# Batch 2's input stage partly by seven block products, with the sums of w_in moved ahead of it

## The chip, the cores and the metric

One core of a Trainium2 chip. The metric is device time in microseconds (us), the median of several executions. The engines work side by side, each through its own list in order: TensorE (PE) multiplies matrices, VectorE (DVE) and ScalarE (ACT) do element work, GpSimd (POOL) does element work and issues DMAs, SyncE (SP) issues DMAs. Only PE writes matmul results, into eight PSUM banks; DVE and ACT read them out into SBUF, where everything else lies. They wait for each other by semaphores.

## The reference

Attention over 4 batches, 8 heads, 768 positions and 64 columns, with a local window of 16 and, for each block of 32 keys, one summary key (the maximum) and one summary value (the mean). Its output, reshaped to 3072 x 512, goes through a dense layer with a quick GELU. Cut to what matters:

```python
k_sum = k.reshape(B, H, nb, block, D).max(axis=3)
v_sum = v.reshape(B, H, nb, block, D).mean(axis=3)
scores_l = where(|i - j| < 16, scale * q @ k.T, -1e9)
scores_s = scale * q @ k_sum.T + log(32)
a = softmax(concat([scores_l, scores_s]))
x = (a @ concat([v, v_sum])).reshape(3072, 512)
h = x @ w_in                                  # 512 x 2048
return (h * sigmoid(1.702 * h)) @ w_out       # 2048 x 512
```

## The kernel before

The four batches run one after the other. Each has an input stage (x @ w_in and the GELU, giving `gT`: 16 tiles of 128 hidden columns, each for two halves of 384 tokens) and an output stage (`gT` @ w_out). Batch b+1's attention is done inside batch b's output stage: `beside` and the table `plan` say after which of the 21 output products which scores, masks, values and transposes stand.

The order is written out by hand. `_Ordered` wraps every engine and pins each instruction to its place in the program, so every engine's list is the order in which the Python code issues the calls. All instructions therefore carry line 28, and have to be told apart by their tiles.

**The output stage** splits w_out, the hidden columns and the tokens into 2 x 2 blocks and computes the four block results with seven products instead of eight (`product`, steps 1 to 7, for three token columns t of 128; `seq` is their order). This needs sums of blocks of `gT` (`g_sums`, four sums `which` 0 to 3 for a pair of tiles j and j+8, into `gs`) and of w_out (`ws`). Evictions: `keep_it` and `give`, on ACT and DVE.

**The input stage** of batches 0 to 2 is plain: for each hidden tile and half, four matmuls of 128x384 (`ff_step`) into a bank of PSUM, then one GELU on ACT (`gelu`). Batch 3's is by seven products for six of eight tile pairs: `win_sum` makes four sums of blocks of w_in (into `wsi`, which lies in the key and query buffers of even batches, `kxs[0]` and `qTs[0]`), `x_sums` four sums of blocks of x (into `xs`, which lies in `vw[0]`), and for each pair j `ff_product` does seven products of two matmuls. Between them stand `ff_copy` "a" (DVE, bank to bank), "s" (ACT, to SBUF), "b" and "c" (DVE, a bank plus the SBUF copy), and four GELUs (`ff_gelu`). `steps` gives the order by slots, and consecutive pairs are seven slots apart. The banks come from `last_bank` by tags A (3 banks), B (1), C (2), E (2).

Since batch 2 is the last even batch, `wsi` and `xs` can be written once its scores and values are done, that is late in batch 1's output stage. Before, the four `win_sum`s stand on DVE at the start of batch 2's input stage (line 1162).

**Also in batch 2's input stage** the keys, values and queries of batch 3 are made ready: on POOL a copy of one column (`gate2`) waits for the last transposed x, then the four DMAs of q are issued (`load_turned`); on SP `xq` transposes q by DMA and `value_rows` copies the halo rows; `vsum` sums the values by blocks on PE (48 small matmuls, `ps_vs`) and DVE copies these sums out; `rest_k` makes the key maxima (`ks`, DVE) and copies them and the halo columns into the key tiles (`key_halos`, `key_rows`, here DVE).

Of the kernel before, what the change touches and what calls it, by code (L numbers as in the profile page):

```python
# [13 lines left out]
ALU = mybir.AluOpType  # L14
# [21 lines left out]
def kernel(  # L36
# [10 lines left out]
    B, H, S, D = q.shape  # L47
# [5 lines left out]
    NP = H // 2  # L53
# [54 lines left out]
    def load_turned(x, b, t2, name, gs_=(0, 1)):  # L108

        for g in gs_:  # L110
            t2[g] = castp2.tile([128, 2, NJ, 2, D], BF16, name=name, tag=name)
            for hh in range(2):
                h0 = hh * NP + 2 * g
                pool.dma_start(out=t2[g][:, :, :, hh].rearrange("p i a d -> p (i a) d"),
                               in_=x[b, h0:h0 + 2].rearrange("h (a p) d -> p (h a) d", p=128))
# [145 lines left out]

    vs_ps = [None]

    def vsum(s):

        if s:
            big = psb.tile([128, 1024], F32, name="ps_vs", tag="big")
            ps = [big[:, 0:512], big[:, 512:1024]]
        else:
            ps = [pmm.tile([128, 512], F32, name="ps_vs", tag="mm") for e in range(2)]  # L270
        vs_ps[0] = ps
        w5 = vw[s].rearrange("p (j e) h c -> p j e h c", e=2)
        for j in range(NJ):
            o = EX - 4 * j
            for g in range(4):
                for e in range(2):
                    pe.matmul(out=ps[e][32 * g:32 * g + 32, 0:2 * D],
                              lhsT=E[e * 64:e * 64 + 64, o:o + 32],
                              rhs=w5[e * 64:e * 64 + 64, j, e, 2 * g:2 * g + 2, 0:D],
                              start=(j == 0), stop=(j == NJ - 1), skip_group_check=True)  # L280
# [348 lines left out]
    def gelu(half, nt, ph):  # L629
        act.activation(out=gT[half][:, nt, :], in_=ph, func=ACT.Gelu_apprx_sigmoid)  # L630
# [3 lines left out]
    def ff_step(ph, half, nt, steps=range(KO)):  # L634
        for n in steps:
            g, i = n // 2, n % 2
            ko = g + 2 * i if halves[0] else 2 * g + i
            pe.matmul(out=ph, lhsT=w_in_sb[:, ko, nt * 128:(nt + 1) * 128],
                      rhs=xTT[half][g][:, i], start=(n == 0), stop=(n == KO - 1))
# [26 lines left out]
        gelu(half, nt, ph)  # L666


    def g_sums(j, eng=dve, which=(0, 2, 1, 3), m=1):

        js = slice(j, j + m)
        a1, a2 = gTb[:, js], gTb[:, j + NT // 2:j + NT // 2 + m]
        l, r = slice(0, HALF), slice(HALF, S)
        for w in which:
            a, b_, op = {0: (a1[:, :, r], a2[:, :, r], ALU.add), 1: (gs[:, 0, js], a1[:, :, l], ALU.subtract),
                         2: (a1[:, :, l], a1[:, :, r], ALU.subtract),
                         3: (a2[:, :, l], gs[:, 1, js], ALU.subtract)}[w]
            eng.tensor_tensor(out=a1[:, :, r] if w == 2 else gs[:, min(w, 2), js], in0=a, in1=b_, op=op)

    N1 = d_model // 2  # L680

# [19 lines left out]
           .rearrange(two, k=2) for i in range(4)]  # L701
    xs = [vflat[:, i * 2 * HALF:(i + 1) * 2 * HALF].rearrange(two, k=2) for i in range(4)]

    def win_sum(what):

        n = NT // 2 * 128
        k1, k2 = w_in_sb[:, K1], w_in_sb[:, K2]
        a11, a12, a21, a22 = k1[:, :, 0:n], k2[:, :, 0:n], k1[:, :, n:], k2[:, :, n:]
        a, b_, op = {0: (a21, a22, ALU.add), 1: (wsi[0], a11, ALU.subtract),
                     2: (a11, a21, ALU.subtract), 3: (a12, wsi[1], ALU.subtract)}[what]  # L710
        dve.tensor_tensor(out=wsi[what], in0=a, in1=b_, op=op)

    def x_sums():

# [6 lines left out]
    def last_bank(tag, name):  # L721
        return plast[tag in "AB"].tile([128, 512], F32, name=name, tag="last" + tag,
                                       bufs={"A": 3, "E": 2, "B": 1, "C": 2}[tag])
# [325 lines left out]
            else:  # L1049
                tx(half, i, XE.get((half, i), act))  # L1050

    def value_rows(s):
        w5 = vw[s].rearrange("p (j e) h c -> p j e h c", e=2)
        halo_dmas(w5, 0)
        vsum(s)
        block_sums()
        sum_dmas(w5, 0)

# [77 lines left out]
    def run1(steps):  # L1136

        for what in steps.split():
# [9 lines left out]
            else:  # L1148
                g_sums(i)

    XB = {0: 'A4 v0 v1 a4 a5 x0 a6 x1 a7 a8', 2: 'b0 b1 z0 b2 b3 z1', 4: 'b4 b5 z2', 6: 'b6 b7 z3', 8: 'b8 a9 b9 z4'}
    for b in range(0, B - 1):
        nxt = b + 1 < B
        s = (b + 1) % 2
        if b == 1:
            mid.close()
            mid = ExitStack()
            pmm = mid.enter_context(tc.tile_pool(name="pmm", bufs=4, space=bass.MemoryType.PSUM, reuse_waits="tile"))
        if b:
            halves[0] = True  # L1160
            if b == B - 2:
                for w in range(4):
                    win_sum(w)
            for n in range(0, NT, 2):
                if b == 1 and n in XB:
                    run1(XB[n])
                elif n == 0:
                    ff_open(0, order2[0:4], None)
                elif n == 2:
                    for nt in order2[0:4]:  # L1170
                        ff_one(1, nt)
                    g_sums(0)
                    g_sums(1)
                else:
                    for nt in order2[n:n + 2]:
                        for half in range(2):
                            ff_one(half, nt)
                        if b == 1 and n + 2 == NT and nt == order2[n]:
                            value_rows(s)
                    g_sums(n // 2, dve, (0, 1) if n + 2 == NT else (0, 1, 2, 3))  # L1180
                if nxt:
                    if n == 0 and b > 1:
                        pool.tensor_copy(out=gate2, in_=xTT[1][1][:, 1, 0:1])
                        load_turned(q, b + 1, qb2, "qb")
                    if b > 1 and n // 2 == 1:
                        xq(0, s)
                        value_rows(s)
                    if b == 1 and n // 2 in (0, 1):
                        xq(n // 2, s)
                    if b > 1 and n // 2 == 2 * b:  # L1190
                        xq(1, s)
                    p = n // 2 - (3 if b == 1 else 2)
                    if 0 <= p < NP:
                        rest_k(p, s, pool if b == 1 else dve)
        if nxt:
            if b:
                exp_soon()
            beside(b + 1, -1)
        i = 0
        for t, what in seq if b else seq0:  # L1200
            product(b, t, what)
            if i == (2 if b else 0):
                g_sums(NT // 2 - 1, dve, (2, 3))
            if nxt:
                beside(b + 1, i)
            i += 1
            if nxt and b + 2 < B:
                if i == 1 and b:
                    load_batch(b + 2)
                if b and i in (16, 18):  # L1210
                    xk(i // 2 - 8, b % 2)

    mid.close()
    mid0.close()
    for ab in (True, False):
        plast[ab] = ctx.enter_context(tc.tile_pool(name=f"plast{ab:d}", bufs=2, space=bass.MemoryType.PSUM,
                                                   reuse_waits="tile"))
    b, n = B - 1, NT // 2
    PLAIN = 2

    def plain(nt, half, tag):
        ph = last_bank(tag, "ph")[:, 0:HALF]
        ff_step(ph, half, nt)
        gelu(half, nt, ph)

    def ff_do(j, what):
        if isinstance(what, int):
            ff_product(j, what)
        elif what in "asbc":
            ff_copy(j, what)  # L1230
        elif what == "g":
            g_sums(j, pool, (0, 1))
        else:
            ff_gelu(j, what)

    for i, tag in enumerate("CCEEAAA"):
        plain((0, n, 1, n + 1)[i % 4], i // 4, tag)
        if i == 3:
            x_sums()
        if i in (5, 6):  # L1240
            g_sums(0, pool, (0, 1) if i == 5 else (2, 3))
    steps = {0: [1, "a"], 1: [5, "s"], 9: [7, "c"], 10: [3], 4: [2], 5: [6, "b"], 13: [4],
             6: ["C"], 11: ["B"], 12: ["E"], 14: ["A"], 15: ["g"]}
    for slot in range(7 * (n - PLAIN)):
        if slot == 1:
            plain(n + 1, 1, "B")
# [53 lines left out]
```

## Time and profile before

| | us |
|---|---|
| median of 3 runs | 207.48 (207.39 to 207.54) |
| the profiled execution | 207.41 |
| its span, first to last instruction | 205.4 |
| batch 2's input stage, first ph to first scores | 120.53 to 142.07 |
| batch 2's output stage | 142.07 to 164.54 |
| batch 3's input stage to the first output product | 164.54 to 182.64 |

How to read it: times are from the start of the span. A row of the chain of waits has a start, a length and the piece of work that the end depended on. A row of the timeline has a start, a length, the engine, the operation, its output and inputs with their shapes, and in brackets the engine's idle time before it and what ended it. PE's rows overlap, since a matmul's end is 0.16 us after the next one's start. The granted TensorE clock was 1.000 throughout.

```profile
120.53:142.07 21.54, 21.54 (x179) 12.81 (x177) 19.85 (x57) 15.24 (x32) 4.79 (x5) 1.00 1.67 164
142.07:164.54 22.47, 22.47 (x362) 19.34 (x361) 14.66 (x32) 12.15 (x21) 0.00 (x0) 1.00 0.41 85
164.54:182.64 18.10, 18.04 (x113) 10.76 (x111) 11.08 (x21) 14.85 (x35) 13.03 (x15) 1.00 0.13 38
```

These are three stretches of the span (start:end, length), with the busy time of PE, PE's weight loads, DVE, ACT and POOL in each, and then the granted clock, the share of the DMA engines and GB/s. They are the input and output stage of batch 2 and the input stage of batch 3.

### The profile page before, as it was taken

How to read it: one execution, taken by the hardware profiler on the slowest of the kernel's cores; microseconds unless marked ns; L12 is line 12 of the kernel's file. 1: busy time of each engine (PE TensorE's matmuls, PEld its weight loads, DVE VectorE, ACT ScalarE, POOL GpSimd, SP SyncE). 2: the span in 40 equal slices, each digit the busy share in tenths (PEclk: the TensorE clock that was granted, in tenths of full speed). 3: DMA queues.
4: the chain of work that ended last, by engine and by line, in shares of the span. 5: the costliest groups of instructions: out<-in, count | busy, mean ns of one | idle time of the engine just before them, and what ended most of it. 6: DMA issues, size and time to landing. Idle time of an engine off the chain costs nothing.

```text
span 205.4 us, 6003 instructions
## 1 busy us (share of the span) xinstructions
PE 196.9 (96%) x2436; PEld 144.6 (70%) x2436; DVE 142.9 (70%) x369; ACT 130.8 (64%) x253; POOL 100.5 (49%) x159
## 2 busy tenths in 40 slices
PE   7879999999999999999999999999999999999993
PEld 7647556656877776656788875666888865668882
DVE  6956875769998544599877579996768446757221
ACT  2373969769788847776772347778680567984220
POOL 7975389944999423746987044000000009991000
PEclk9999999999999999999999999999999999999999
DMA  5999999999999999999999999999023940000222
GB/s 56 160 156 198 200 209 209 193 158 136 83 164 192 207 189 196 134 126 150 114 165 204 187 155 154 169 210 147 3 102 89 135 140 0 2 3 0 102 105 102
DMA packets 99723, 27.75 MB, mean 135 GB/s; under 512 B 86752, under 2 KB 96752, under 8 KB 99696
## 3 DMA queue, kind: packets, MB, share of 16 engines
q0 software_dynamic: 74064, 13.64, 89.1%
q1 hardware_dynamic: 25632, 13.74, 35.4%
q8 instruction: 19, 0.31, 0.7%
q14 instruction: 8, 0.07, 0.1%
HBM read 27.26 MB, written 6.29 MB: 163 GB/s over the span
## 4 chain that ended last, share of the span: by engine, by line
PE 59%; DMA 15%; POOL 13%; DVE 8%; issue 2%; ACT 0%; POOLq 0%; DVEq 0%
PE poA L28 18%; PE ph L28 16%; DMA qb<-in_q_dram 9%; PE poB L28 9%; DMA w_in_sb<-in_moe_w_in_dram 6%; PE poC L28 4%; PE phA L28 4%; DVE gs L28 4%; POOL kb L28 3%; PE ps_av L28 3%; PE ps_s L28 2%; POOL mk L28 2%; POOL v0n L28 2%; DVE ks L28 2%; POOL qb L28 2%
## 5 line engine op out<-in xcount | busy, mean ns | idle before, releaser
L28 PE MATMUL ph<-xT,w_in_sb 128*128 128x384 f16 x416 | 71.1, 326 | 0.1
L28 PEld LDWEIGHTS <-w_in_sb 128*128 128x128 f16 x452 | 43.3, 98 | 27.6 <-issue 0.5
L28 ACT ACTIVATE gT<-ph 128x384 f16<-128x384 f32 x104 | 49.6, 491 | 18.9 <-PE ph L28 18.6
L28 PEld LDWEIGHTS <-gT 128*128 128x128 f16 x384 | 36.1, 98 | 5.3 <-issue 0.2
L28 POOL DMA_DIRECT2D vw<-in_v_dram x36 | 25.1, 752 | 19.4 <-DMA qb<-in_q_dram 7.5
L28 PEld LDWEIGHTS <-gs 128*128 128x128 f16 x288 | 27.7, 98 | 3.6 <-issue 0.3
L28 ACT ACTIVATE a_sb<-ps_s 128x768 bf16<-128x768 f32 (+1 forms) x32 | 24.8, 826 | 7.8 <-PE ps_s L28 7.8
L28 POOL TENSOR_TENSOR gs<-gT 128x384 f16<-128x384 f16 x7 | 6.4, 910 | 43.7 <-ACT gT L28 43.7
L28 PE MATMUL poA<-ws,gT 128*128 128x256 f16 x192 | 25.1, 273 | 0.1
L28 DVE TENSOR_TENSOR a_sb<-a_sb,mk 128x768 bf16<-128x768 bf16 x28 | 14.6, 554 | 5.5 <-ACT a_sb L28 2.8
L28 POOL DMA_DIRECT2D qb<-in_q_dram x18 | 16.6, 945 | 2.5 <-DMA v0n<-in_v_dram 2.2
L28 DVE TENSOR_TENSOR x<-ps_av,rc 128x768 f16<-128x768 f32 (+1 forms) x20 | 15.8, 797 | 0.6
L28 POOL DMA_DIRECT2D kb<-in_k_dram x16 | 15.3, 973 | 0.8 <-POOLq L1284 0.8
L28 ACT ACTIVATE osb<-poA 128x256 f32<-128x256 f32 x12 | 4.6, 384 | 16.1 <-PE poA L28 16.0
L28 ACT ACTIVATE s<-poA 128x256 f32<-128x256 f32 x17 | 6.5, 384 | 12.6 <-PE poA L28 12.1
L28 DVE TENSOR_TENSOR gs<-gT 128x384 f16<-128x384 f16 (+1 forms) x22 | 8.8, 399 | 8.0 <-ACT gT L28 7.8
L28 PEld LDWEIGHTS <-kx 64*128 64x128 bf16 (+1 forms) x372 | 9.4, 95 | 6.5 <-issue 4.2
L28 ACT ACT_TABLE_LOAD x10 | 12.8, 1283 | 1.0 <-PEq L1284 0.8
L28 PE MATMUL poA<-ws,gs 128*128 128x256 f16 x96 | 12.4, 273 | 0.1
L28 PE MATMUL poA<-w_out_sb,gT 128*128 128x256 f16 x96 | 12.5, 273 | 0.0
L28 PE MATMUL poB<-ws,gs 128*128 128x256 f16 x96 | 12.5, 273 | 0.0
L28 PE MATMUL poC<-w_out_sb,gT 128*128 128x256 f16 x96 | 12.5, 273 | 0.0
(113 smaller groups left out, 299.7 us busy)
## 6 DMA issues: line engine op xcount, KB each, us to landing
out_dram<-osb SPq DMA_DIRECT2D x23, 256.0 KB, 4.1
kb<-in_k_dram POOLq DMA_DIRECT2D x16, 192.0 KB, 7.9
qb<-in_q_dram POOLq DMA_DIRECT2D x14, 192.0 KB, 9.9
vw<-in_v_dram POOLq DMA_DIRECT2D x36, 64.0 KB, 7.1
w_out_sb<-in_moe_w_out_dram POOLq DMA_DIRECT2D x3, 512.0 KB, 10.7
vw<-vs SPq DMA_DIRECT2D x6, 198.0 KB, 5.9
w_in_sb<-in_moe_w_in_dram POOLq DMA_DIRECT2D x4, 256.0 KB, 10.0
w_in_sb<-in_moe_w_in_dram POOLq DMA_DIRECT2D x2, 512.0 KB, 12.0
```

Source lines behind the costliest of these rows:

```text
L28: r = f(*a, **kw)
```

## The change

Batch 2's input stage gets a function of its own, `middle`. Tile pairs 0, 1, 6 and 7 stay plain; pairs 2 to 5 go by seven products, with the helpers of batch 3 and the slot table `steps2`. PSUM is handed out by `last_bank` for this stage, and the pools of before are opened again behind it.

- `win_sum` takes an engine. Its four calls move into batch 1's output stage (`WSUM`): sum 0 on DVE after product 10, sum 2 on POOL after product 13, sum 1 on DVE after 15, sum 3 on POOL after 16. POOL's stand behind batch 3's key and value loads and ahead of the gate copy and the q loads.
- `x_sums` is also called at the start of `middle`, behind the last evictions of batch 1. `value_rows` stands behind the first 16 matmuls and gets two E banks for its sums (`vsum` takes `ps`).
- `rest_k`'s copies go to POOL; the maxima stay on DVE, at the slots in `REST`.
- `g_sums` takes a range of token columns. In `middle` only those of column t = 0 are made (`G0`: pairs 0 and 1, 2 to 4, 5 to 7, all on DVE); those of t = 1 and 2 stand in batch 2's output stage, for all eight pairs at once (`OUTG`, 128x1024 each).
- The lists of ACT and DVE change to match: ACT gets four copies "s", DVE four each of "a", "b" and "c".

```diff
+    OUTG = {1: [(1, 0)], 2: [(1, 1)], 3: [(1, 2)], 4: [(1, 3)], 7: [(2, 0)], 8: [(2, 1)], 9: [(2, 2)], 10: [(2, 3)]}
+    WSUM = {10: [(0, 0)], 13: [(2, 1)], 15: [(1, 0)], 16: [(3, 1)]}
+    LEAD, SEVEN, TAIL = [0, 1], [2, 3, 4, 5], [6, 7]
+    steps2 = {0: [1, "a"], 1: [5, "s"], 4: [2], 5: [6, "b", "C"], 9: [7, "c"], 10: [3], 11: ["B"], 12: ["E"], 13: [4], 14: ["A"]}
+    REST, TAILS, G0 = {6: 0, 12: 1, 20: 2, 27: 3}, {6: 1, 9: 1, 13: 1, 16: 1, 20: 1, 27: 1, 30: 1, 33: 1}, {3: [(0, 2, (0, 2, 1, 3), 0)], 29: [(2, 3, (0, 1), 0)], 31: [(2, 3, (2, 3), 0)], 33: [(5, 3, (0,), 0)], 35: [(5, 3, (1, 2, 3), 0)]}
+
+    def middle(b, s):
+        n = NT // 2
+        pool.tensor_copy(out=gate2, in_=xTT[1][1][:, 1, 0:1])
+        load_turned(q, b + 1, qb2, "qb")
+        tags = iter('CCAACCCB')
+        nts = [nt for j in LEAD for nt in (j, j + n)]
+        phs = {nt: last_bank(next(tags), "ph")[:, 0:HALF] for nt in nts}
+        for part in ((0, 1), (2, 3)):
+            for nt in nts:
+                ff_step(phs[nt], 0, nt, part)
+        for nt in nts:
+            gelu(0, nt, phs[nt])
+        x_sums()
+        xq(0, s)
+        value_rows(s, [last_bank("E", "ps_vs") for e in range(2)])
+        for nt in nts[:-1]:
+            plain(nt, 1, next(tags))
+        more = iter([(h, nt) for j in TAIL for nt in (j, j + n) for h in range(2)])
+        tails = iter('CCCCCCAA')
+        for slot in range(7 * len(SEVEN) + 9):
+            if slot == 1:
+                plain(nts[-1], 1, next(tags))
+            for k_, j in enumerate(SEVEN):
+                for what in steps2.get(slot - 7 * k_, ()):
+                    if what != "g":
+                        ff_do(j, what)
+            for i in range(TAILS.get(slot, 0)):
+                h, nt = next(more)
+                plain(nt, h, next(tails))
+            for j, m, which, eng in G0.get(slot, ()):
+                g_sums(j, (dve, pool)[eng], which, m, 0, 1)
+            if slot in REST:
+                rest_k(REST[slot], s, pool)
+            if slot == 10:
+                xq(1, s)
...
         if b:
             halves[0] = True
             if b == B - 2:
-                for w in range(4):
-                    win_sum(w)
+                mid.close()
+                mid0.close()
+                mid, mid0 = ExitStack(), ExitStack()
+                last_pools(mid)
+                middle(b, s)
...
         for t, what in seq if b else seq0:
             product(b, t, what)
-            if i == (2 if b else 0):
+            if b < B - 2 and i == (2 if b else 0):
                 g_sums(NT // 2 - 1, dve, (2, 3))
+            for t_, w in OUTG.get(i, ()) if b == 2 else ():
+                g_sums(0, dve, (w,), NT // 2, t_, t_ + 1)
+            for w, eng in WSUM.get(i, ()) if b == 1 else ():
+                win_sum(w, (dve, pool)[eng])
             if nxt:
                 beside(b + 1, i)
```

The other lines of the diff make room for this: `vsum` and `g_sums` take their new arguments, `plain`, `ff_do`, `steps` and `last_pools` move up unchanged in what they do, and batch 2's cases leave the common loop over tiles.

More of the change, by code (lines that the diff above doesn't have):

```diff
@@ L262, with vsum @@
     vs_ps = [None]
-    def vsum(s):
-        if s:
+    def vsum(s, ps=None):
+        if ps:
+            pass
+        elif s:
             big = psb.tile([128, 1024], F32, name="ps_vs", tag="big")
@@ L666, in ff_one, with g_sums @@
         gelu(half, nt, ph)
-    def g_sums(j, eng=dve, which=(0, 2, 1, 3), m=1):
+    def g_sums(j, eng=dve, which=(0, 2, 1, 3), m=1, t0=0, t1=JH):
         js = slice(j, j + m)
         a1, a2 = gTb[:, js], gTb[:, j + NT // 2:j + NT // 2 + m]
-        l, r = slice(0, HALF), slice(HALF, S)
+        l, r = slice(t0 * 128, t1 * 128), slice(HALF + t0 * 128, HALF + t1 * 128)
         for w in which:
-            a, b_, op = {0: (a1[:, :, r], a2[:, :, r], ALU.add), 1: (gs[:, 0, js], a1[:, :, l], ALU.subtract),
+            a, b_, op = {0: (a1[:, :, r], a2[:, :, r], ALU.add), 1: (gs[:, 0, js, l], a1[:, :, l], ALU.subtract),
                          2: (a1[:, :, l], a1[:, :, r], ALU.subtract),
-                         3: (a2[:, :, l], gs[:, 1, js], ALU.subtract)}[w]
-            eng.tensor_tensor(out=a1[:, :, r] if w == 2 else gs[:, min(w, 2), js], in0=a, in1=b_, op=op)
+                         3: (a2[:, :, l], gs[:, 1, js, l], ALU.subtract)}[w]
+            eng.tensor_tensor(out=a1[:, :, r] if w == 2 else gs[:, min(w, 2), js, l], in0=a, in1=b_, op=op)
     N1 = d_model // 2
@@ L702, with win_sum @@
     xs = [vflat[:, i * 2 * HALF:(i + 1) * 2 * HALF].rearrange(two, k=2) for i in range(4)]
-    def win_sum(what):
+    def win_sum(what, eng=dve):
         n = NT // 2 * 128
@@ L710, in win_sum @@
                      2: (a11, a21, ALU.subtract), 3: (a12, wsi[1], ALU.subtract)}[what]
-        dve.tensor_tensor(out=wsi[what], in0=a, in1=b_, op=op)
+        eng.tensor_tensor(out=wsi[what], in0=a, in1=b_, op=op)
     def x_sums():
@@ L1050, in beside, with value_rows @@
                 tx(half, i, XE.get((half, i), act))
-    def value_rows(s):
+    def value_rows(s, ps=None):
         w5 = vw[s].rearrange("p (j e) h c -> p j e h c", e=2)
         halo_dmas(w5, 0)
-        vsum(s)
+        vsum(s, ps)
         block_sums()
@@ L1149, in run1, with plain, ff_do @@
                 g_sums(i)
+    PLAIN = 2
+    def plain(nt, half, tag):
+        ph = last_bank(tag, "ph")[:, 0:HALF]
+        ff_step(ph, half, nt)
+        gelu(half, nt, ph)
+    def ff_do(j, what):
+        if isinstance(what, int):
+            ff_product(j, what)
+        elif what in "asbc":
+            ff_copy(j, what)
+        elif what == "g":
+            g_sums(j, pool, (0, 1))
+        else:
+            ff_gelu(j, what)
+    steps = {0: [1, "a"], 1: [5, "s"], 9: [7, "c"], 10: [3], 4: [2], 5: [6, "b"], 13: [4],
+             6: ["C"], 11: ["B"], 12: ["E"], 14: ["A"], 15: ["g"]}
@@ new lines, in last_pools @@
+    def last_pools(stack):
+        for ab in (True, False):
+            plast[ab] = stack.enter_context(tc.tile_pool(name=f"plast{ab:d}", bufs=2, space=bass.MemoryType.PSUM,
+                                                         reuse_waits="tile"))
+    OUTG = {1: [(1, 0)], 2: [(1, 1)], 3: [(1, 2)], 4: [(1, 3)], 7: [(2, 0)], 8: [(2, 1)], 9: [(2, 2)], 10: [(2, 3)]}
+    WSUM = {10: [(0, 0)], 13: [(2, 1)], 15: [(1, 0)], 16: [(3, 1)]}
+    LEAD, SEVEN, TAIL = [0, 1], [2, 3, 4, 5], [6, 7]
+    steps2 = {0: [1, "a"], 1: [5, "s"], 4: [2], 5: [6, "b", "C"], 9: [7, "c"], 10: [3], 11: ["B"], 12: ["E"], 13: [4], 14: ["A"]}
@@ L1161 @@
             if b == B - 2:
-                for w in range(4):
-                    win_sum(w)
-            for n in range(0, NT, 2):
+                mid.close()
[3 more added lines that the diff above has]
+                middle(b, s)
+                mid.close()
+                mid = ExitStack()
+                pmm = mid.enter_context(tc.tile_pool(name="pmm", bufs=4, space=bass.MemoryType.PSUM,
+                                                     reuse_waits="tile"))
+                psb = mid0.enter_context(tc.tile_pool(name="psb", bufs=2, space=bass.MemoryType.PSUM, side="right",
+                                                      reuse_waits="tile"))
+            for n in range(0, NT if b < B - 2 else 0, 2):
                 if b == 1 and n in XB:
@@ L1181 @@
                 if nxt:
[L1182 to L1188, printed above, removed]
-                        xq(n // 2, s)
[L1190 to L1194, printed above, removed]
+                    if n // 2 in (0, 1):
+                        xq(n // 2, s)
+                    if 3 <= n // 2 < 3 + NP:
+                        rest_k(n // 2 - 3, s, pool)
         if nxt:
@@ L1214 @@
     mid0.close()
-    for ab in (True, False):
-        plast[ab] = ctx.enter_context(tc.tile_pool(name=f"plast{ab:d}", bufs=2, space=bass.MemoryType.PSUM,
-                                                   reuse_waits="tile"))
+    last_pools(ctx)
     b, n = B - 1, NT // 2
[L1219 to L1234, printed above, removed]
     for i, tag in enumerate("CCEEAAA"):
@@ L1241 @@
             g_sums(0, pool, (0, 1) if i == 5 else (2, 3))
-    steps = {0: [1, "a"], 1: [5, "s"], 9: [7, "c"], 10: [3], 4: [2], 5: [6, "b"], 13: [4],
-             6: ["C"], 11: ["B"], 12: ["E"], 14: ["A"], 15: ["g"]}
     for slot in range(7 * (n - PLAIN)):
```

## The prediction

> **What bounds the kernel now.** I read four views, in this order: busy time by engine, the chain of waits in order of time around batch 2, the rows of VectorE (DVE), GpSimd (POOL) and the SP queue in time over the stretch that the change touches, and the landing times of the DMAs there, from the semaphores in the trace.
>
> ```profile
> PE 196.9 (96%) x2436; PEld 144.6 (70%) x2436; DVE 142.9 (70%) x369; ACT 130.8 (64%) x253; POOL 100.5 (49%) x159
> ```
>
> Here only the PE share matters: 96% of the span. The chain says whether this is work or waiting.
>
> ```profile
> 119.83 0.87 PE poA L28 x8
> 120.70 5.20 PE ph L28 x32
> 125.90 0.53 PE ps_vs L28 x48
> 126.43 15.71 PE ph L28 x96
> 142.14 0.46 PE ps_s L28 x24
> ```
>
> From the last product of batch 1 (119.83) to the first scores of batch 3 (142.14) no piece but PE's own stands in the chain: batch 2's input stage is 128 matmuls, end to end, at 5.20 / 32 = 0.1625 us each, and the 48 small value sums. So a matmul taken out is worth 0.1625 us as long as nothing else comes late. The question is what comes late.
>
> ```profile
> 111.93 0.96 DVE L28 TENSOR_TENSOR x<-ps_av,rc 128x768 f16<-128x768 f32 x1
> 115.54 0.96 DVE L28 TENSOR_TENSOR x<-ps_av,rc 128x768 f16<-128x768 f32 x1
> 118.17 0.42 DVE L28 TENSOR_TENSOR osb<-poC,s 128x256 f32<-128x256 f32 x1 [1.68 <-PE poC L28]
> 120.27 1.22 DVE L28 TENSOR_TENSOR kx<-w_in_sb 128x2048 f16<-128x2048 f16 x1
> ...
> 110.70 2.71 POOL L28 DMA_DIRECT2D vw<-in_v_dram  x4 [0.31 <-DMA vw<-in_v_dram]
> 120.75 0.78 POOL L28 CAST gate<-xT 128x1 bf16<-128x1 f16 x1 [7.33 <-DMA xT<-x]
> 121.47 4.06 POOL L28 DMA_DIRECT2D qb<-in_q_dram  x4
> ...
> 184.82 0.91 POOL L28 TENSOR_TENSOR gs<-gs,gT 128x384 f16<-128x384 f16 x1
> ...
> 185.26 0.68 DVE L28 TENSOR_TENSOR gs<-gT 128x384 f16<-128x384 f16 x1 [0.66 <-ACT gT L28]
> 185.98 0.36 DVE L28 TENSOR_TENSOR gs<-gs,gT 128x384 f16<-128x384 f16 x1
> ...
> 138.12 2.20 SPq L28 DMA_TRANSPOSE qT<-qb  x1
> ```
>
> The reader should see that POOL is idle from 113.41 (110.70 + 2.71) to 120.75; that DVE has one free stretch of 1.68 us at 116.5; and that a DVE sum of two SBUF operands took 0.68 instead of 0.36 us when it met a POOL sum. That sum ended at 185.94, 0.21 after POOL's (185.73): it waited for POOL's end with 0.15 of its own time already done.
>
> **The change, part by part.**
>
> *Matmuls.* Four plain tile pairs (16 matmuls each) become four of 14: 128 to 120, so 8 x 0.1625 = 1.30 us less. Loads of weights go with them.
>
> *Two sums of w_in on DVE in batch 1's output stage.* Sum 0 (1.22) stands after the product at 109.99, ahead of the reciprocal at 110.53. That delays the second normalization, which ended at 112.89 (111.93 + 0.96), by about 0.96, to 113.85. PE's second half of the next values product needs that buffer and its weights at about 113.9: I count 0.1 us of stall. Sum 1 falls into the free stretch before 118.17.
>
> *Two sums on POOL, the unknown price.* No row shows a POOL sum of 128x2048. POOL's 128x384 sum takes 0.91, its one-column copy 0.19. If none of the 0.91 is a fixed part, 2048 columns take 0.91 x 2048/384 = 4.85; if all of the 0.19 is fixed, 0.19 + 0.72 x 2048/384 = 4.03. I take 4.5, near the middle, and keep both ends. POOL starts sum 2 at 113.41 and ends it at 117.9. Sum 1 on DVE, ready to start at 116.8, has two SBUF operands; by the 0.68 row it is held to 117.75 and ends at 119.0. The evictions behind it on DVE (poC, then poA, about 0.34 apart) then end at 119.3 and 119.65. Product 4 of the last tile column, at PE's 119.66 row, waits for the second of these: just in time, no cost. If the cover goes, each 0.1 us that POOL takes longer costs PE 0.1 here.
>
> Sum 3 waits for sum 1 and runs from 119.1 to 123.6. Now x_sums (four DVE sums of two SBUF operands) meet it: by the same row they are held to 123.45, though their input lands at about 121. Four of them take 2.05 (in batch 3 they are 0.56 long, 0.47 apart), to 125.45; the five operations on the value sums take 1.2, to 126.65, and the copy "a" of the first seven-product pair 0.57 (batch 3's row), to 127.2. On PE, product 2 follows 16 matmuls (2.60), the value sums (0.53), 12 (1.95), 2, 4 and 2 more (1.30): 120.70 + 6.38 = 127.1, plus the delays counted here. So this too fits by a hair. Beyond 4.5 a second 0.1 is lost here for each 0.1, since both POOL sums are in this path. At 4.85, 0.5 us is lost in all.
>
> The Trainium skill (SBUF — State Buffer, Who interferes with whom) says that a Vector instruction with two SBUF inputs and a GpSimd instruction that reads SBUF share a port pair, and the one that starts first holds the other off for its whole length. The 0.68 row agrees, and so does the one-column POOL copy: 0.19 alone, 0.78 beside DVE's w_in sum at 120.27, which ended at 121.49 as that copy ended at 121.53. Without this rule, sum 1 and x_sums would run at 116.8 and 121, and the sum would be the same 1.0 us of gain at any POOL price up to 4.85.
>
> The skill's GPSIMD Engine Reference (3.1 Elementwise) gives 4497 ns for a GpSimd sum of 2048 fp32 elements and advises to leave such work to the Vector engine. As an estimate for f16 that is the same 4.5, and the sum by it is the same.
>
> *The seven-product steps.* They are batch 3's own, whose stage runs on PE with one hole of 0.23 (at 171.7). Two things differ. Plain tiles share two banks of tag C: from the last matmul of one tile to its free bank is 0.33 + 0.04 + 0.49 + 0.05 = 0.91, and the next-but-one tile wants it 0.81 after: 0.1 lost, once. And DVE puts four short sums (1.1) ahead of the first "b", which holds product 7: 0.1. ACT gets 4 copies of 0.49 more and 1.3 us less of time, at 15.24 busy of 21.54 in this stage: covered.
>
> *Moved from the stage to elsewhere.* The key copies go from DVE (4 x 0.5) to POOL, idle then. Two thirds of batch 2's g_sums (8 sums of 128x1024, 0.65 each by 1.35 for 2304) go into the output stage, where DVE is busy 14.66 of 22.47: 5.2 more. Only those ahead of the first normalization at 154.54 push: about 1.2 there, which moves the next normalizations past PE's values product by 0 to 0.2, and the last transposes of x (landing at 165.83, wanted at 167.3) by 0.7. I take nothing, and 0.2 for the range.
>
> *The q loads of batch 3* stand on POOL behind both sums. They go from 121.47 to about 124.2 (sum 3 to 123.6, then the gate copy, held by the first x sum): 2.7 later. On SP they hold the first q transpose, the halo copies and sum rows, then the second transpose, which was issued at 138.12 and by its semaphore landed at 143.28. Scores at 146.12 read it, at 145.1 after the change. Slack 1.8, shift at most 2.7: bounds 0 and 0.9. I take 0, because the q loads shared the rings with four k transposes (issued from 119.25) that will be nearly through by then.
>
> Sum: -1.30 + 0.1 + 0.1 + 0.1 = -1.0 us. The profiled execution took 207.41 (span 205.4, 2.0 around it), so 206.4 for it; the median of the runs is 207.48, 0.07 above. I forecast **206.5**.
>
> **Rivals.**
>
> 1. *The POOL sum is as dear as its elements: 4.85.* For it, the 0.91 row scaled; against, a fixed part is likely. 0.5 lost: 207.0. Chance 0.14.
> 2. *The q chain moves as a whole.* For: one queue, each step waits for the one before. Against: the SP queue, not the landing, set 138.12, and the rings are emptier. 0.9 lost: 207.4, and 208 if the transposes take longer as well. Chance 0.15.
> 3. *Slower: POOL's sums are stretched by DVE.* For: POOL's three key copies of one head pair took 0.75 at 60.8, with no two-operand sum on DVE, and 1.11 to 1.18 beside its g_sums at 91 to 96, half as much again; a 2048-column sum at 1.35 times 4.5 is 6.0. Against: 18 POOL sums of 0.91 in batch 3 show no spread while DVE works out of PSUM. Beyond 4.55 each 0.1 costs 0.2, so from 5.05 on the gain is gone; 6.0 costs 2.9: 209.4. Chance 0.08.
> 4. *No gain: DVE becomes the bound of batch 2's stage.* From 123.45 it has x_sums 2.05, value sums 1.2, twelve a/b/c at 0.49, four key maxima at 0.87 and 12 short sums of about 0.25, in all 15.6 us, of the 17.6 up to 141. Against: 2 us are left. If its order makes PE wait 0.1 at each of eight steps more, 0.8 goes: 207.3. Chance 0.07.
>
> **How the numbers follow.** Forecast 0.56 (its own range 206.2 to 206.8: nothing lost at all to twice the small terms). The range is 206.1 to 207.6: the low end is all of the 1.30 with the spread of the runs, the high end takes in rivals 1 and 4 and most of 2, and leaves rival 3 and the end of 2 out. Less than 0.2% (0.41 us) can't be told from no change here. Faster (under 207.07): the forecast and most of rival 1, 0.68. Same: part of rival 1, half of 2, rival 4, 0.17. Slower (over 207.9): rival 3, part of 2, 0.15.
>
> **What would show it.** PE should have 2428 matmuls, and the stretch from the first ph of batch 2 to the first scores of batch 3 should be about 20.5 us instead of 21.5. POOL's two sums: 4.0 to 4.6 each means the cover holds; the DVE sum 1 should start late and its row end about 1.2 after POOL's sum 2. x_sums should start where sum 3 ends. A PE hole ahead of product 4 at 119.7 or ahead of phC at 127 speaks for rivals 1 and 3; a hole ahead of the scores of the third head pair for rival 2; many holes of 0.1 before phA and phC for rival 4. I am wrong if the POOL sums last over 5 us or the second q transpose lands after 145.

## The result and the profile after

The changed kernel takes 206.41 us (median of 22 runs, 205.45 to 209.8), the kernel before 207.23 on the same chip (22 runs, 206.57 to 208.48). The ratio is 0.9951, with a 95% interval of 0.9933 to 0.9970. Two more comparisons of the same two kernels gave 0.9949 (0.9922 to 0.9975) and 0.9942 (0.9914 to 0.9970). So it is faster by about half a per cent, some 1.0 to 1.2 us of 207 by these ratios, and no interval reaches less than 0.25%. The ratios are estimates over all runs and not quotients of the medians; by the medians alone the gain is 0.8 us here. The forecast was 206.5 and a gain of 1.0.

Runs that were longer at a lower granted clock (of the changed kernel's 22 those of 209.8 us at 0.947 and 208.54 at 0.992) are left out of the ratios and of the medians in the table further down, and as the first of them was the profiled one, the profile shown is of the third comparison (`e1b_after`, 207.11 us, span 205.1, clock 1.000). It is 1.0 us above the median of its kernel there, while the profile before was 0.2 above that of its own. So the two profiles are compared by stages and not by their spans: the spread arises ahead of the changed stage, as the experiments show.

From the page of `e1b_after`, busy time by engine:

```profile
PE 196.9 (96%) x2428; PEld 144.4 (70%) x2428; DVE 147.1 (72%) x355; ACT 130.9 (64%) x257; POOL 113.0 (55%) x177
```

PE has the 2428 matmuls, eight fewer. POOL has taken over 12.5 us of work (100.5 before). The same two stretches as before, in the windows view of `e1b_after` (batch 2's input stage, batch 2's output stage; columns as before):

```profile
121.04:141.75 20.71, 20.55 (x170) 12.00 (x169) 17.42 (x33) 14.89 (x36) 11.10 (x22) 1.00 1.55 158
141.75:164.22 22.47, 22.47 (x361) 19.34 (x361) 18.88 (x42) 12.49 (x23) 0.00 (x0) 1.00 0.53 101
```

The input stage fell from 21.54 to 20.71 us: 0.83 less. The output stage is 22.47 as before, though DVE works 18.88 us in it and not 14.66: the moved sums of gT are hidden whole. From batch 3's first ph to the last product it is 36.54 us before and 36.55 after. So the gain lies in this one stage, and 20.55 of 20.71 says that PE waited a little there. Where, the chain of waits of `e1b_after` says:

```profile
126.80 0.66 PE ph L28 x4
...
127.49 0.50 ACT gT L28
...
128.01 0.50 DVE gs L28
...
129.27 0.57 DVE phB L28
...
129.88 0.48 PE phA L28 x2
...
141.82 0.46 PE ps_s L28 x24
```

Before, this chain was PE's alone. Now it leaves PE once in this stage: a GELU, four short sums of gT on DVE, the first copy "b" (phB), and only then product 7 (phA at 129.88, with a hole of 0.31 ahead of it). The two engines at the start of the stage, in the timelines of POOL and DVE of `e1b_after`:

```profile
113.76 4.12 POOL L28 TENSOR_TENSOR kx<-w_in_sb 128x2048 f16<-128x2048 f16 x1
119.05 4.06 POOL L28 TENSOR_TENSOR qT<-w_in_sb,kx 128x2048 f16<-128x2048 f16 x1 [1.17 <-DVE kx L28]
...
127.57 0.78 POOL L28 COPY kx<-kx 128x80 bf16<-128x80 bf16 x3
...
117.19 1.78 DVE L28 TENSOR_TENSOR kx<-kx,w_in_sb 128x2048 f16<-128x2048 f16 x1
...
120.83 2.69 DVE L28 TENSOR_TENSOR vw<-xT,xT 128x768 f16<-128x768 f16 x1
123.56 0.56 DVE L28 TENSOR_TENSOR vw<-xT,vw 128x768 f16<-128x768 f16 x1
...
128.01 0.49 DVE L28 TENSOR_TENSOR gs<-gT 128x256 f16<-128x256 f16 x1 [0.54 <-ACT gT L28]
128.53 0.29 DVE L28 TENSOR_TENSOR gT<-gT 128x256 f16<-128x256 f16 x1
```

The POOL sums last 4.12 and 4.06. DVE's sum 1 ends at 118.97, 1.09 after POOL's sum 2 (117.88). The first x sum takes 2.69 where the next takes 0.56, and ends at 123.52, 0.41 after POOL's sum 3 (123.11). The same at a small scale: the first short gT sum takes 0.49 where the next takes 0.29, because the last of POOL's three key copies (127.57 to 128.35 together; the last is one of 128x192, from 127.96) stands beside it; it ends 0.15 after that copy.

### The profile page after: what moved, and what is told of

It is laid out like the page before. It is cut to its first block, busy times and chain, and to the rows that moved or that the text cites. A ratio compares the mean times of both kernels' runs of the same rounds, so it can differ in the third digit from the quotient of the medians.

```text
span 207.8 us, 5998 instructions
## 1 busy us (share of the span) xinstructions
PE 200.4 (96%) x2428; PEld 145.7 (70%) x2428; DVE 147.8 (71%) x355; ACT 131.0 (63%) x257; POOL 112.9 (54%) x177
## 4 chain that ended last, share of the span: by engine, by line
PE 78%; POOL 9%; DMA 6%; DVE 4%; issue 2%; ACT 0%; POOLq 0%; DVEq 0%
PE ph L28 23%; PE poA L28 20%; PE poB L28 10%; PE phA L28 6%; DMA w_in_sb<-in_moe_w_in_dram 6%; PE poC L28 5%; PE ps_av L28 3%; PE ps_s L28 3%; POOL mk L28 2%; POOL v0n L28 2%; PE phC L28 2%; PE phB L28 2%; PE phE L28 1%; PE ps_t L28 1%; POOL kb L28 1%
## 5 line engine op out<-in xcount | busy, mean ns | idle before, releaser
L28 PE MATMUL ph<-xT,w_in_sb 128*128 128x384 f16 x352 | 64.3, 334 | 0.1
L28 PEld LDWEIGHTS <-w_in_sb 128*128 128x128 f16 x412 | 40.0, 99 | 26.5 <-issue 0.2
L28 ACT ACTIVATE gT<-ph 128x384 f16<-128x384 f32 x88 | 41.9, 492 | 19.7 <-PE ph L28 19.1
L28 PE MATMUL poA<-ws,gT 128*128 128x256 f16 x192 | 25.6, 277 | 0.0
L28 PEld LDWEIGHTS <-kx 64*128 64x128 bf16 (+1 forms) x396 | 11.8, 96 | 8.2 <-issue 4.0
L28 DVE TENSOR_TENSOR gs<-gT 128x384 f16<-128x384 f16 (+3 forms) x19 | 8.6, 453 | 7.6 <-ACT gT L28 7.4
L28 POOL COPY kx<-ks 128x288 bf16<-128x288 bf16 x11 | 4.8, 440 | 16.5 <-DVE ks L28 16.5
```

What stands on the lines that cost most here:

```text
L28: r = f(*a, **kw)
```

## The experiments

Executions of one kernel spread over some 2 us (205.6 to 207.36 in `e1_after`), and the profiles show where: the first ph of batch 2, with no hole ahead of it, stands anywhere from 119.9 to 121.1 us, though the program up to there is nearly the same in all. From the first scores behind the stage to the end of the span, all of them have 63.3 to 63.5 us, less the holes listed as behind it. Medians of some 12 runs therefore tell 0.5 us apart at best, while the length of the stage in the profile is much finer: the two profiles of the changed kernel differ by 0.02. This table is read with each experiment. All times in us; "stage" is from the first ph of batch 2 to the first scores behind it. Holes under 0.1 are left out; every kernel with the new stage has one of 0.09, at the bank of tag C.

| kernel | median (runs) | ratio to before | stage | holes on PE |
|---|---|---|---|---|
| before | 207.13 (34) | | 21.54 | none |
| e3_sums | 206.98 (12) | 0.9987 (0.9964 to 1.0010) | 21.53 | none |
| e2_plain | 207.86 (12) | 1.0030 (1.0003 to 1.0056) | 21.62 | 0.62 behind it |
| e2b_plain | 207.07 (11) | 1.0004 (0.9971 to 1.0038) | 21.62 | 0.21 behind it |
| e1_after | 206.42 (12) | 0.9949 (0.9922 to 0.9975) | 20.69 | 0.30 at product 7, 0.98 behind it |
| e1b_after | 206.11 (8) | 0.9942 (0.9914 to 0.9970) | 20.71 | 0.31 at product 7 |
| e5_sum3dve | 206.51 (12) | 0.9968 (0.9939 to 0.9996) | 20.92 | 0.18 and 0.27 at products 7, 0.14 at the last product |
| e6_memset | 206.25 (12) | 0.9967 (0.9941 to 0.9993) | 20.52 | 0.12 at product 7 |
| e7_order | 206.66 (12) | 0.9957 (0.9933 to 0.9981) | 20.33 | none |
| e9_dve | 206.48 (12) | 0.9956 (0.9930 to 0.9981) | 20.33 | none |
| e10_late | 206.84 (12) | 0.9976 (0.9950 to 1.0002) | 20.59 | 0.68 ahead of it, 0.20 at product 7 |
| e8_five | 207.89 (12) | 1.0034 (1.0008 to 1.0060) | 21.78 | 0.78 ahead of it, 0.26 to 0.56 four times |
| e4_twice | 210.83 (4) | 1.0163 (1.0125 to 1.0200) | 25.83 | 0.41 ahead of it, 2.30 and 1.49 in it |

The kernel before was run beside each of three groups: its median was 207.13 beside e1, e2, e3 and e5, 207.03 beside e2b, e6, e7 and e8, and 207.14 beside e1b, e4, e9 and e10.

### The changed kernel again

> The changed kernel once more, for an undisturbed profile and a second comparison with the kernel before. Theory (the stage is bound by its matmuls, and the two POOL sums stay within their cover): 0.7 to 1.3 us faster than before; POOL's two sums 4.0 to 4.2 each; DVE's sum 1 ends 1.0 to 1.2 after POOL's sum 2, the first x sum ends 0.3 to 0.5 after POOL's sum 3; no hole on PE of over 0.15 between batch 1's last product and the first scores of batch 3. Rival (the gain comes from somewhere else, such as the output stage): the stretch from the first ph of batch 2 to the first scores of batch 3 stays above 21.2 us.

The gain, POOL's sums and the holds came as the theory had them. Two things did not: the hole of 0.30 at product 7, where none over 0.15 was expected, and a hole of 0.98 behind the stage, where the scores of the third head pair read the second q transpose. First the timelines of the SP queue and of PE in `e1_after`, then the landing of that transpose in the view of its tile:

```profile
138.71 3.35 SPq L28 DMA_TRANSPOSE qT<-qb  x1
...
146.01 0.53 PE L28 MATMUL ps_s<-qT,kx 64*128 64x64 bf16 x24 [0.98 <-DMA qT<-qb]
```

```profile
DMA to landing us min/median/max: 7.2/7.2/7.2
```

The transpose landed 7.2 us after its issue, at 145.9; before it was 5.2. That is rival 2 of the prediction to the size (0.9), and past the 145 at which the prediction had said that it would be wrong, so it was tested by itself, below.

### The seven products undone, the rest kept

> The changed kernel with pairs 2 to 5 of batch 2 plain again, all else as changed: w_in's sums in batch 1's output stage, x_sums early, the key copies on POOL, two thirds of g_sums in the output stage. Theory (the eight matmuls saved are the gain, and every other part is worth about nothing): 1.0 to 1.4 us slower than the changed kernel, so within 0.3 us of the kernel before, with 2436 matmuls. Rival (the moved sums, which take 5 us off DVE in this stage, bring the gain): within 0.4 us of the changed kernel.

```diff
+        PL = {0: [(0, 0)], 4: [(1, 0)], 9: [(0, 1)], 13: [(1, 1)]}
...
-                for what in steps2.get(slot - 7 * k_, ()):
-                    if what != "g":
-                        ff_do(j, what)
+                for h, up in PL.get(slot - 7 * k_, ()):
+                    plain(j + up * n, h, "AE"[h])
```

In this version sum 0 of pairs 5 to 7 reads the right half of tile 13 before its GELU writes it, and the GELU then waits for the sum: that is the hole of 0.62. With it the median is 0.7 above the kernel before, so "within 0.3" was missed. The second version has 12 where this one has 13:

> As e2_plain, with the last plain tile of pair 5 one slot earlier, ahead of the sum that reads it. In e2_plain that sum stood first, so the last GELU waited for it and PE had a hole of 0.62 ahead of its first scores. Theory (the eight matmuls are the gain): 0.6 to 1.0 us slower than the changed kernel, within 0.3 of the kernel before, and no hole ahead of the first scores. Rival (something else in the changed order costs or gains): off from the kernel before by more than 0.4.

It came out at 1.0004 of the kernel before, with a stage of 21.62 and no hole ahead of the first scores. So the eight matmuls are the gain, and the rest of the change gains nothing by itself: in the profile it costs the 0.09 at tag C's bank, and here a hole of 0.21 behind the stage.

### The sums of w_in alone

> The kernel before with one part of the change alone: the four sums of w_in in batch 1's output stage, two on DVE and two on POOL at the changed kernel's places, batch 2's input stage plain as before. Theory: no more than 0.2 us from the kernel before, either way: the sums are off the path there, and the price of sum 0 ahead of the second normalization is at most 0.1. Rival (sum 0 stalls PE by most of the 0.96 that it delays the normalization): 0.6 to 1.0 us slower than before.

```diff
+    WSUM = {10: [(0, 0)], 13: [(2, 1)], 15: [(1, 0)], 16: [(3, 1)]}
...
-            if b == B - 2:
-                for w in range(4):
-                    win_sum(w)
...
+            for w, eng in WSUM.get(i, ()) if b == 1 else ():
+                win_sum(w, (dve, pool)[eng])
```

0.9987, and the stage is 21.53: nothing gained and nothing lost. From the first of the two values products in batch 1's output stage to the first ph of batch 2 it is 10.62 us here and 10.61 in the profiles before and after (109.92 to 120.53; 109.60 to 120.21 in `e1_after`). Sum 0 ahead of the second normalization stalls PE by nothing.

### Sum 3 on DVE, and POOL's extra time that only writes

> The changed kernel with sum 3 of w_in on DVE, directly ahead of the sums of x, and not on POOL. POOL then issues the q loads of batch 3 about 3 us earlier, and DVE is held by nobody. Theory (the late q loads and the held x sums both fit in their slack): within 0.2 us of the changed kernel; the first x sum ends no later than it did. Rival 1 (the q loads are late in the changed kernel): 0.3 to 0.9 us faster than it. Rival 2 (DVE has no room for 1.2 us more at this place): 0.4 to 1.2 us slower.

```diff
-    WSUM = {10: [(0, 0)], 13: [(2, 1)], 15: [(1, 0)], 16: [(3, 1)]}
+    WSUM = {10: [(0, 0)], 13: [(2, 1)], 15: [(1, 0)]}
...
+        win_sum(3)
         x_sums()
```

> The changed kernel with four writes of a constant to a scratch of 128x1024 on POOL behind sum 3, ahead of the gate copy: some us more on POOL that read nothing from SBUF, L in all. Theory (the q chain of batch 3 has no slack left behind sum 3: in e1_after its second q transpose landed at 145.87, and the third head pair's scores stood 0.98 for it): these scores wait longer, by about L, the time grows by 0.7 to 1.0 times L, and the x sums end where they did. Rival (the 0.98 was chance in that execution, there is slack of 1 or 2 us): the time grows by less than half of L.

```diff
+                if w == 3:
+                    for _ in range(4):
+                        pool.memset(scratch, 0.0)
```

With sum 3 on DVE the x sums are done 1.1 us earlier (123.41, in `e1_after` 124.53) and the q loads start 1.4 earlier (121.62 and 122.99); the median stays within 0.1 of `e1_after`, so the hold was hidden, as the theory says. Its stage is 0.2 longer all the same, by the three holes in the table. The writes delayed the q loads by 3.2 us instead, and cost nothing either: the theory that the q chain has no slack fell. First the timelines of POOL, DVE, SP and PE of `e6_memset`, then the landing of its four q loads in the view of their tile on POOL:

```profile
122.13 3.99 POOL L28 MEMSET scratch<- 128x1024 f16 x4
...
126.19 4.10 POOL L28 DMA_DIRECT2D qb<-in_q_dram  x4
...
123.12 0.55 DVE L28 TENSOR_TENSOR vw<-xT,xT 128x768 f16<-128x768 f16 x1
...
140.26 1.60 SPq L28 DMA_TRANSPOSE qT<-qb  x1
...
144.48 0.53 PE L28 MATMUL ps_s<-qT,kx 64*128 64x64 bf16 x24
```

```profile
DMA to landing us min/median/max: 5.7/6.5/7.1
```

The q loads landed 5.7 to 7.1 us after their issue, in `e1_after` 6.2 to 10.2. The k transposes were nearly through when they started: these landed 3.3 to 4.2 us after their issue, where in `e1_after`, with q loads beside the last two, it was 4.0 to 9.0. So the last q load, issued 3.2 later, landed only 0.15 later (at 136.39 and 136.24 by its semaphore). The second q transpose was issued 1.55 later than in `e1_after` and landed after 4.1 us, at 144.3, just in time for the scores. Counted from the first ph that is 24.5 us, between the two profiles of the changed kernel (25.7 in `e1_after`, 23.6 in `e1b_after`). And the writes held off nobody: the x sum at 123.12 has its plain 0.55 beside them.

### Where the rest of the stage is lost, and one pair more

> e5_sum3dve (sum 3 on DVE) with two moves on DVE more: the four short sums of pairs 0 and 1 from slot 3, ahead of the first b, to slot 17, and two sums of pairs 2 to 4 from slot 29, ahead of the last c, to slot 30, behind it. Theory (what is left in this stage are holes ahead of product 7, 0.30 and 0.27 in the profiles, and the late q loads): the holes at about 129.0 and 138.9 go, the stretch from the first ph to the first scores is 20.3 to 20.5 us, no hole ahead of the scores of the third head pair; 0.2 to 0.7 us faster than the changed kernel, 1.0 to 1.5 faster than before. Rival (these holes only let DVE or ACT catch up and come back later): within 0.2 us of e5_sum3dve, stretch 20.7 or more.

```diff
-    REST, TAILS, G0 = {6: 0, 12: 1, 20: 2, 27: 3}, {6: 1, 9: 1, 13: 1, 16: 1, 20: 1, 27: 1, 30: 1, 33: 1}, {3: [(0, 2, (0, 2, 1, 3), 0)], 29: [(2, 3, (0, 1), 0)], 31: [(2, 3, (2, 3), 0)], 33: [(5, 3, (0,), 0)], 35: [(5, 3, (1, 2, 3), 0)]}
+    REST, TAILS, G0 = {6: 0, 12: 1, 20: 2, 27: 3}, {6: 1, 9: 1, 13: 1, 16: 1, 20: 1, 27: 1, 30: 1, 33: 1}, {17: [(0, 2, (0, 2, 1, 3), 0)], 30: [(2, 3, (0, 1), 0)], 31: [(2, 3, (2, 3), 0)], 33: [(5, 3, (0,), 0)], 35: [(5, 3, (1, 2, 3), 0)]}
```

> e7_order with pair 6 by seven products too, five of eight: two matmuls less (2426), one more copy on ACT and one a, b and c more on DVE, and the sums of pairs 2 to 7 some slots later. Theory (PE still bounds the stage): 0.2 to 0.33 us faster than e7_order. Rival (DVE bounds it by now): same as e7_order or up to 0.5 slower, with holes of 0.1 to 0.3 ahead of products 7 and of phC.

```diff
-    LEAD, SEVEN, TAIL = [0, 1], [2, 3, 4, 5], [6, 7]
+    LEAD, SEVEN, TAIL = [0, 1], [2, 3, 4, 5, 6], [7]
...
-        tails = iter('CCCCCCAA')
+        tails = iter('CCCC')
```

`TAILS` keeps slots 6, 13, 20 and 27, and the short sums of pairs 2 to 7 stand four to seven slots later. The windows view of the stage, first of `e7_order`, then of `e8_five`:

```profile
121.14:141.47 20.33, 20.33 (x171) 12.03 (x169) 16.28 (x34) 14.83 (x36) 9.10 (x21) 1.00 1.61 164
```

```profile
121.41:143.19 21.78, 20.63 (x168) 11.80 (x166) 17.22 (x37) 15.82 (x37) 8.79 (x21) 1.00 1.57 171
```

In `e7_order` the holes are gone but for the 0.09 at tag C's bank, and the stage is 20.33: 1.21 less than before, of 1.30 that the matmuls are worth. The median doesn't show the 0.38 against `e1b_after`: it is 0.2 to 0.6 above those of the changed kernel, beside other runs of before, and the intervals overlap. So the expected faster time was not shown. With a fifth pair the stage grows by 1.45: DVE and ACT do about one us more, and DVE's copies now come late at four steps (holes of 0.26 and 0.48 ahead of phC, 0.56 and 0.49 ahead of phA). The median is 1.2 above that of `e7_order`, more than theory or rival had. Four pairs are what this order carries; no other order of five pairs was run. Its 0.78 ahead of the stage is another matter, next.

### The cover of POOL's sums

> The changed kernel with one write of a constant to a scratch of 128x1024 on POOL ahead of sum 2: sum 2 starts and ends 1.0 us later. Theory (beyond its cover each 0.1 us of POOL costs PE 0.1 at product 4 of batch 1's last column, and part of that again ahead of phC): sum 1 on DVE ends 1.0 later, PE has a hole of 0.6 to 1.0 there, and the time grows by 0.7 to 1.6 us. Rival (sum 1 has 1 us or more of slack): no hole, time within 0.2 of the changed kernel.

```diff
+                if w == 2:
+                    pool.memset(scratch, 0.0)
```

> e7_order with sum 1 too on DVE ahead of the x sums, so that POOL makes sum 2 alone, which then holds off nobody. Theory (the cover of POOL's sums was thin, and an execution whose value loads let POOL start late pays for it; DVE has 1.0 + 0.4 us idle ahead of the copy a): no hole in batch 1's last products, none over 0.15 ahead of phC, stretch 20.2 to 20.5 us, 0 to 0.5 faster than the changed kernel. Rival (DVE is now late with the x sums and the value sums): a hole of 0.2 to 0.8 ahead of phC, and a time up to 0.5 above e7_order.

```diff
-    WSUM = {10: [(0, 0)], 13: [(2, 1)], 15: [(1, 0)]}
+    WSUM = {10: [(0, 0)], 13: [(2, 1)]}
...
+        win_sum(1)
         win_sum(3)
```

The timelines of POOL and DVE of `e10_late`:

```profile
113.36 4.12 POOL L28 TENSOR_TENSOR kx<-w_in_sb 128x2048 f16<-128x2048 f16 x1
...
115.65 2.93 DVE L28 TENSOR_TENSOR kx<-kx,w_in_sb 128x2048 f16<-128x2048 f16 x1
...
118.84 0.41 DVE L28 TENSOR_TENSOR osb<-poA,s 128x256 f32<-128x256 f32 x1
```

Sum 1 is held until 118.58, 1.10 after POOL's 117.48, the eviction of poA behind it ends at 119.25, and the last product into poA starts at 119.30, 0.68 late. Of the profiles with sum 1 at this place, two more had this hole with no write added, and in both POOL's value loads had waited 1.8 to 1.9 us for earlier loads (`e4_twice` and `e8_five`). Counted from the end of POOL's sum 2 to the place where the first ph would stand without the hole:

| | e1b | e5 | e2b | e3 | e6 | e1 | e7 | e4 | e10 | e8 |
|---|---|---|---|---|---|---|---|---|---|---|
| us left | 3.16 | 3.10 | 3.04 | 2.97 | 2.91 | 2.86 | 2.78 | 2.26 | 2.01 | 1.90 |
| hole | 0 | 0 | 0 | 0 | 0 | 0 | 0 | 0.41 | 0.68 | 0.78 |
| sum | | | | | | | | 2.67 | 2.69 | 2.68 |

The hole is what is missing to 2.68 us, 0.1 for 0.1 (`e2_plain`, with 3.17 left, had none either). The median of `e10_late` is 0.7 above that of `e1b_after`, which ran beside it. Ahead of phC there was no second hole, though the expectation had one. The changed kernel's margin in its profiles is 0.2 to 0.5. In `e9_dve` 2.19 us were left and there was no hole, since sum 1 isn't there to be held; its x sums were in time too, and its stage 20.33. In the median it is not told apart from the changed kernel, so the gain of a safer place is shown in the profile alone.

### Once more the changed kernel, and the hold itself

> The changed kernel a third time, beside the next three on the same chip. Theory (the 0.98 us at the scores of the third head pair in e1_after came from crowded DMA rings in that execution and not from the place of the q loads): the profile has no hole there or one under 0.3, the stretch from the first ph of batch 2 to the first scores is 20.5 to 20.8 us, and the median 0.5 to 1.2 below the kernel before. Rival (the late q loads cost it every time): again 0.7 to 1.2 there.

> The changed kernel with sum 3 of w_in issued twice in a row on POOL, 4.1 us more there that read SBUF, where e6_memset had 4.0 us that only wrote. Theory (a POOL sum holds off DVE's sums of two SBUF operands for its whole length): the x sums end about 4 us later than the changed kernel's, near 128.5, the copy a of the first seven-product pair too, PE gets a hole of 3 to 4 us ahead of product 2 (phC), and the time grows by 3 to 4 us. Rival (the x sums wait for something else, such as their data): they end at 124.5, and as with e6_memset the time stays within 0.3 of the changed kernel.

```diff
-    WSUM = {10: [(0, 0)], 13: [(2, 1)], 15: [(1, 0)], 16: [(3, 1)]}
+    WSUM = {10: [(0, 0)], 13: [(2, 1)], 15: [(1, 0)], 16: [(3, 1), (3, 1)]}
```

`e1b_after` had no hole at the third head pair's scores: its second q transpose landed after 5.3 us, at 144.6, and was wanted at 145.8. Of the profiles with sum 3 on POOL (`e3_sums`, `e2_plain`, `e2b_plain`, `e1_after`, `e1b_after`, `e6_memset`, `e10_late`, `e4_twice`) only `e1_after` waited there. What crowded the DMA rings in that one execution, the profiles don't say; it stays open how often it happens.

POOL, DVE and PE in `e4_twice`, and the windows view of the stretch behind PE's holes:

```profile
118.94 8.40 POOL L28 TENSOR_TENSOR qT<-w_in_sb,kx 128x2048 f16<-128x2048 f16 x2 [1.17 <-DVE kx L28]
...
123.44 4.30 DVE L28 TENSOR_TENSOR vw<-xT,vw 128x768 f16<-128x768 f16 x1
127.67 0.54 DVE L28 TENSOR_TENSOR vw<-xT,xT 128x768 f16<-128x768 f16 x1
...
130.80 0.73 PE L28 MATMUL phC<-xT,w_in_sb 128*128 128x384 f16 x2 [1.33 <-DVE phC L28]
```

```profile
130.91:134.32 3.41, 3.41 (x12) 1.64 (x11) 2.49 (x7) 0.98 (x2) 2.23 (x7) 0.50 2.28 145
```

DVE got one x sum in between the two POOL sums, and the next was held for 4.30 us, to 0.40 after POOL's end (127.34). The same 4 us on POOL cost nothing where they only wrote, and 4.7 in the median here (210.83 and 206.11). That is more than the 3 to 4 expected. The hold gave what was foreseen: the copy "a" comes 3.9 later behind the first ph than in `e1b_after`, and PE has holes of 2.30 and 1.49. The rest is PE itself: behind the second hole the granted clock was 0.50 for 3.41 us, the matmuls stood 0.32 apart and not 0.16, and 1.7 us went there. Another 0.41 is POOL's late sum 2.

The Trainium skill (SBUF — State Buffer, Who interferes with whom) adds that a Vector instruction with two SBUF inputs does not contend with a GpSimd instruction that only writes SBUF. `e6_memset` agrees: 0.55 beside the writes.

## Why the prediction was right, point by point

**The matmuls.** 8 x 0.1625 = 1.30, and as PE bounds the stage it came in full, less what PE waited: 21.54 - 1.30 + 0.09 (tag C) + 0.31 (the first "b") + 0.09 (two small holes, 0.04 at 131.2 and 0.05 at 141.3) = 20.73, measured 20.71. The 20.5 forecast for the stage was 0.2 too low: the stage gained 0.83 and not 1.0. That the time still came within 0.1 of the 206.5 is in part luck. The forecast started from a median of 207.48 in three runs, which was 207.23 in 22, and this 0.25 hid that the gain is smaller (0.8 by the medians, 1.0 by the ratio).

**Tag C's bank that waits for a GELU**: 0.1 forecast, 0.09 measured, at 125.67 in `e1b_after`.

**The first "b" behind four short sums** was mis-sized: 0.1 forecast, 0.30 and 0.31 measured. In `e6_memset`, where POOL's key copies came later, it was 0.12. So 0.2 of it is the price of "The key copies go from DVE (4 x 0.5) to POOL, idle then": POOL was idle, but its copies held off a short sum on DVE (the first in `e1b_after`, the third in `e1_after`, 0.43 long), just as the large sums did.

**Sum 0 ahead of the second normalization**: 0.1 forecast, 0.00 measured. The delay was right (the normalization ended 0.96 later against PE, at 113.53 in `e1_after`), but no stall came: the values product that it was to hold starts 3.60 behind the one before it, as it did before (3.61).

**The last copy "c"**, which stood behind two sums of pairs 2 to 4, cost 0.05, one of the two small holes. The prediction didn't have it.

**POOL's sums.** 4.06 to 4.12, near the lower bound of 4.03, as if most of the 0.19 of the one-column copy were a fixed part. As 4.5 was taken, there was a margin of 0.2 to 0.5 where the forecast had none. The estimate from the Trainium skill (GPSIMD Engine Reference, 3.1 Elementwise) had been the same 4.5, from its 4497 ns for fp32; in f16 the traces show 4.06 to 4.12. The point from which it costs was right: POOL's end at 117.9 in the times of before is 2.63 us ahead of the first ph at 120.53, measured 2.68. The price of 0.1 for 0.1 at the eviction was right too. The second 0.1 ahead of phC stays open. In `e10_late` POOL started 1.0 later, sum 3 and PE slid together, and there was no hole there; but longer sums, which the prediction meant, would delay sum 3 twice and PE once, and were not run. Rivals 1 and 3 rested on that doubled slope and on POOL sums of 4.85 and 6.0; neither length was seen.

**The q loads.** Against PE they moved by 1.8 (`e1_after`: 2.78 behind the first ph, before 0.94) and 1.5 (`e1b_after`: 2.47), not by 2.7, since sum 3 ended earlier. Their cost of 0 holds in all profiles but one. The reason given, that loads which start later find emptier rings, is what `e6_memset` shows for loads that start later still. Rival 2 came true once, 0.98, with the transpose landing at 145.9, past the prediction's own limit of 145; as `e6_memset` has no such hole with still later loads, their place alone doesn't cause it.

**Moved sums of gT**: 0, as forecast; the output stage is 22.47 in both. **Rival 4**, DVE as the bound, is not this kernel's but the next step's: with five pairs, in the one order run, DVE's copies come late.

## What to carry to other kernels

An engine that has time is not free if its instructions hold off those of a busy one: before work is moved to POOL, look which DVE instructions beside it read two operands from SBUF, and put it next to those that read PSUM, or next to none. Here the two normalizations out of PSUM beside POOL's sum 2 kept their 0.96 us, while sum 1 went from 1.22 to 1.78 and more. The price of such a hold is counted from the cover: 2.68 us here, nothing above it and 0.1 for 0.1 below. When executions spread by more than the change is worth, compare the stage's length in the profiles first and the medians for the sign.

## What was not expected of the hardware

- A hold works between small instructions too: a POOL copy of 128x192, 0.38 long, stretched a DVE sum of 128x256 from 0.29 to 0.49.
- POOL that only writes (128x1024 f16, 1.0 us each) held no DVE sum.
- The second q transpose landed 4.1 to 7.2 us after its issue, and the last k transpose after 3.5 us where the q loads were issued behind it (`e6_memset`) and 9.0 where they started ahead of it (`e1_after`).
- In `e4_twice` the granted clock was 0.50 for 3.41 us right behind two PE holes of 2.30 and 1.49. One profile shows it; behind holes under 1 us, as in `e8_five`, the clock stayed at 1.00.
